# Where chunk 0 of the MLP passes into chunk 1: operands, sums, residual loads and stores in other places, and w2 at other addresses

## The chip, the cores and the metric

The kernel runs on one core of a Trainium2 chip. The metric is the device time of one execution in microseconds. Before the change it is 1118.84 us, the median of three runs (1115.59, 1118.84 and 1119.8 us).

## What is computed

A Performer attention layer feeds a two-layer MLP with a residual. The reference, cut to what matters:

```python
# q, k, v: 8 batches, 8 heads, 576 tokens, 64 wide; omega: 128 x 64
h = x @ omega.T - sum(x * x) / 2          # for x = scaled q and scaled k
phi = exp(h - max(h)) / sqrt(128)
attn = (q_p @ (k_p.T @ v)) / (q_p @ sum(k_p) + 1e-6)
x = attn                                   # 8 x 576 x 512
u = x + ((x.T @ U) @ V).T                  # U: 576 x 32, V: 32 x 576
out = u + relu(u @ w_ch1) @ w_ch2          # 512 -> 2048 -> 512
```

The change touches only the last line.

## The kernel before

The MLP's 4608 tokens are 36 tiles of 128 rows, taken in nine **chunks**: chunk 0 has six tiles, chunks 1 to 7 have four, chunk 8 has two. Every float32 product is made of three TensorE matmuls, from a high and a low half of each operand (`split`: ScalarE rounds the high half, GpSimd or VectorE subtracts it to get the low half). TensorE (PE) is fed in an order that the program fixes, and so are the other engines in this part (`keep`).

**Chunk 0** runs in `whole_pass`: for each of the 16 blocks f of w1's 2048 columns, 24 matmuls of the first layer (L853, twelve of 512 columns and twelve of 256), then 18 of the second layer (L927: six tiles t, three matmuls each, against the tiles `w2h` and `w2l` of block f), while `each(f, i)`, for i = 0 to 3, hangs other work between them: the decoder that turns the stored float64 weights into float32 (`raw` loads, `mag`, `low`, `w2h`, `w2l`), and towards the end the preparation of chunk 1. Its inputs come from DRAM by `fetch` (`uraw`, four DMAs each on SP's queue), are turned by VectorE (L792, `uT`), summed by GpSimd (L822, `us`) and split into `ux`.

**Chunks 1 to 7** do the first layer with seven products in place of eight (`products`), over blocks p and p + 8 of w1: eight **passes** p = 0 to 7 for each chunk, each of seven **units** i = 0 to 6 of six 256-column matmuls (L901, into the banks X, Y, Z and W). The operands of a pass are seven `wx` tiles, made of blocks of w1 and of four VectorE sums `ws` (`Weights.add`); in chunk 1 they are made and stored to DRAM (`wx_dram`), later chunks load them back (`Again`). After a unit VectorE and ScalarE combine the banks (`near`, `far`) and apply the relu (`g`). The second layer of one pass is a generator `steps` of single matmuls (L927), which the next pass takes one by one between its own: 24 of them, and 18 in the first pass of chunk 1, which carries the end of chunk 0. Z is in bank p_m and W in p_kv; chunk 0 ends with its tiles 4 and 5 in the same two banks, so the `store` of these tiles (L946: VectorE adds the residual `u` that L941 loaded) has to be done before units 2 and 5 of the first pass. Unit 3 accumulates on unit 0's bank, unit 4 on unit 1's, unit 6 on unit 2's: unit 6 may start when VectorE has read Z for `far` (c22, after unit 4).

Before, `pairs` (the operands of chunk 1's first pass) get four of their seven tiles in chunk 0's f = 14 and one in f = 15, and the residuals of chunk 0 are loaded in f = 14. `between(i)`, after each unit, then adds one operand of the running pass and one of the next. `prepare`, the three GpSimd sums of the next chunk, stands whole behind unit 6 of pass 6.

In SBUF, w2's blocks 0 and 1 start at addresses with remainder 128 by 256 and its blocks 2 to 15 at remainder 224; `g`, `ux` and `wx` start at 160.

## Time and profile before

| | us |
|---|---|
| median of three runs | 1118.84 |
| the profiled execution's own time | 1119.64 |
| its span (first to last instruction) | 1117.9 |
| TensorE busy | 1088.7 (97%) |
| attention, up to about 360 us | 360.00 with 343.72 of TensorE busy |
| chunk 8, from 1062.7 us | 55.30 with 51.48 of TensorE busy |

The first and the last third of the profile are outside of the change. A matmul's busy time (0.28 us for 256 columns, 0.40 us for 512) is longer than the spacing of two starts, because matmuls overlap; time lost is therefore read from the spacing of starts. A bracket such as [2.34 <-DVE g L862] is the idle time ahead of an instruction and what ended it.

### The profile page before, as it was taken

The page shows a single profiled execution, that of the slowest core. Times are in us where ns is not written, and L with a number is a line of the kernel's source. Part 1 is how long each engine was busy: PE and PEld are TensorE (multiplying, and loading weights), DVE is VectorE, ACT ScalarE, POOL GpSimd, SP SyncE. Part 2 cuts the span into 40 slices and gives each one's busy share as a digit, 9 for nine tenths or more (in the row PEclk, how much of TensorE's full clock was granted, in tenths as well). Part 3 has the DMA queues.
Part 4 walks back from the last instruction along what each step waited for, and adds up shares of the span by engine and source line. Part 5 has one row for each costly group of instructions (what it writes and reads, how often), then busy time and mean ns, then how long its engine had stood idle before and what let it go on. Part 6 is the DMA issues. An engine that isn't in the chain of part 4 may idle for free.

```text
span 1117.9 us, 20593 instructions
## 1 busy us (share of the span) xinstructions
PE 1088.7 (97%) x7105; PEld 981.6 (88%) x7105; DVE 686.5 (61%) x1487; ACT 501.5 (45%) x1405; POOL 325.9 (29%) x337
## 2 busy tenths in 40 slices
PE   8999999999979998999999999999999999999998
PEld 7899889999958887789889989999999999999987
DVE  3899998988987775465743643644644644643421
ACT  4889879898845664334412212222222222222232
POOL 3446647445234554445400100100100100100133
PEclk8999999999989999989999999999999999999999
DMA  7779876674434462375695695785795795785510
GB/s 131 147 149 158 167 172 133 151 143 86 105 87 132 134 166 41 116 252 179 203 269 159 213 265 162 209 269 161 208 270 162 207 271 162 208 260 165 179 58 19
DMA packets 344360, 187.93 MB, mean 168 GB/s; under 512 B 275872, under 2 KB 275872, under 8 KB 344256
## 3 DMA queue, kind: packets, MB, share of 16 engines
q1 hardware_dynamic: 344192, 186.55, 63.2%
q8 instruction: 57, 0.93, 0.3%
q14 instruction: 47, 0.39, 0.1%
q0 software_dynamic: 64, 0.07, 0.0%
HBM read 152.99 MB, written 33.55 MB: 167 GB/s over the span
## 4 chain that ended last, share of the span: by engine, by line
PE 78%; DVE 9%; ACT 4%; DMA 3%; issue 2%; POOL 2%; SPq 2%; DVEq 0%; POOLq 0%; ACTq 0%
PE p_s L901 24%; PE p_n L927 16%; PE p_q L927 14%; PE p_p L853 4%; PE p_kv L442 4%; PE p_n L488 4%; PE p_p L530 3%; PE p_p L531 2%; PE p_p L532 2%; PE p_q L468 2%; POOL mag L164 1%; PE py L327 1%; DVE mag L143 1%; DVE mag L140 1%; SPq L383 1%
## 5 line engine op out<-in xcount | busy, mean ns | idle before, releaser
L901 PEld LDWEIGHTS p_s<-ux,wx 128*128 128x128 f32 x2352 | 443.2, 189 | 65.5 <-issue 3.1
L901 PE MATMUL p_s<-ux,wx 128*128 128x256 f32 x2352 | 472.3, 283 | 6.3 <-DVE far L706 3.5
L927 PE MATMUL p_n<-w2h,g 128*128 128x512 f32 x576 | 213.3, 396 | 0.0
L927 PE MATMUL p_q<-w2h,g 128*128 128x512 f32 x512 | 199.0, 394 | 0.0
L545 ACT ACTIVATE e<-p_p,nm 128x128 f32<-128x128 f32 x576 | 167.1, 386 | 36.2 <-DVE nm L538 28.4
L411 POOL TENSOR_TENSOR xl<-xT,xh 128x384 fp32r<-128x384 f32 x96 | 100.8, 1067 | 132.9 <-ACT xh L407 114.0
L822 POOL TENSOR_TENSOR us<-uT 128x512 f32<-128x512 f32 x14 | 19.2, 1370 | 338.5 <-DVE uT L792 338.5
L861 ACT ACTIVATE g<-far 128x256 fp32r<-128x256 f32 x112 | 46.8, 418 | 157.1 <-DVE far L706 157.1
L706 DVE TENSOR_TENSOR near<-p_s,near 128x256 f32<-128x256 f32 x168 | 70.3, 419 | 74.7 <-PE p_s L901 71.8
L927 PE MATMUL p_n<-w2l,g 128*128 128x512 f32 x288 | 113.8, 395 | 0.0
L703 POOL TENSOR_TENSOR wx<-w1f,wx 128x256 fp32r<-128x256 f32 x88 | 68.6, 795 | 153.6 <-DMA u<-u_dram 81.6
L538 DVE TENSOR_REDUCE nm<-p_p 128x4 f32<-128x512 f32 x144 | 98.0, 681 | 23.6 <-PE p_p L532 16.0
L927 PEld LDWEIGHTS p_n<-w2h,g 128*128 128x128 f32 x576 | 105.4, 190 | 4.5
L861 ACT ACTIVATE g<-p_s 128x256 fp32r<-128x256 f32 x56 | 21.6, 385 | 186.1 <-PE p_s L901 186.1
L853 PEld LDWEIGHTS p_p<-ux,wx 128*128 128x128 f32 x576 | 87.9, 193 | 15.0 <-DVE g L862 3.8
L927 PE MATMUL p_q<-w2l,g 128*128 128x512 f32 x256 | 100.7, 393 | 0.0
L853 PE MATMUL p_p<-ux,wx 128*128 128x256 f32 (+1 forms) x576 | 97.6, 323 | 3.0 <-DVE g L862 3.0
L862 DVE SCALAR_TENSOR_TENSOR g<-p_s,g 128x256 fp32r<-128x256 f32 x56 | 23.7, 424 | 124.9 <-ACT g L861 124.6
L927 PEld LDWEIGHTS p_q<-w2h,g 128*128 128x128 f32 x512 | 96.6, 189 | 3.0
L530 PE MATMUL p_p<-omh,xh 128*128 128x256 f32 x288 | 93.2, 324 | 2.0 <-ACT e L545 1.7
L862 DVE SCALAR_TENSOR_TENSOR g<-far,g 128x256 fp32r<-128x256 f32 x112 | 49.8, 445 | 54.2 <-ACT g L861 54.2
L532 PE MATMUL p_p<-omh,xl 128*128 128x256 f32 x288 | 81.7, 284 | 0.0
(122 smaller groups left out, 1882.9 us busy)
## 6 DMA issues: line engine op xcount, KB each, us to landing
wx<-wx_dram SPq DMA_DIRECT2D x336, 256.0 KB, 3.3
raw<-in_moe_w_ch_dram SPq DMA_DIRECT2D x32, 512.0 KB, 4.0
wx_dram<-wx SPq DMA_DIRECT2D x56, 256.0 KB, 2.4
u_dram<-ut SPq DMA_DIRECT2D x36, 256.0 KB, 2.2
u<-u_dram SPq DMA_DIRECT2D x34, 256.0 KB, 4.4
out_dram<-u SPq DMA_DIRECT2D x34, 256.0 KB, 3.2
kt<-in_k_dram SPq DMA_DIRECT2D x120, 72.0 KB, 2.8
qt<-in_q_dram SPq DMA_DIRECT2D x120, 72.0 KB, 2.7
```

The costliest lines, as they stand in the source:

```text
L411: nc.gpsimd.tensor_tensor(out=self.xl[-1], in0=self.turned, in1=f32(self.xh[-1]), op=ALU.subtract)
L530: nc.tensor.matmul(o, part.xh[g][:, ts], oh, start=True, stop=False)
L532: nc.tensor.matmul(o, part.xl[g][:, ts], oh, start=False, stop=True)
L538: nc.vector.tensor_reduce(out=self.nm[:, :n], in_=self.pp[:, :n], axis=AX.X, op=ALU.max, negate=True)
L545: nc.scalar.activation(out=self.e[:, j, :], in_=self.pp[:, j, :], func=AF.Exp, bias=self.nm[:, j : j + 1])
L703: keep(rest.tensor_tensor(out=hl[:, 1], in0=x, in1=f32(hl[:, 0]), op=SUBTRACT))
L706: keep(nc.vector.tensor_tensor(out=out, in0=a, in1=b, op=op))
L853: nc.tensor.matmul(ph, l, r, start=(cc + i == 0), stop=(cc == NC - 1 and i == 2))
L861: keep(nc.scalar.activation(out=g[:, 0, ts], in_=x, func=AF.Relu))
L862: keep(nc.vector.scalar_tensor_tensor(out=g[:, 1, ts], in0=x, scalar=0.0, in1=f32(g[:, 0, ts]), op0=ALU.max, op1=ALU.subtract))
L901: tc.keep_in_program_order(nc.tensor.matmul(o, l, r, start=(i in (0, 1, 2, 5) and k + j == 0), stop=(k == 1 and j == 2), skip_group_check= ...
L927: tc.keep_in_program_order(nc.tensor.matmul(po, l, r, start=(begin and n + i == 0), stop=(end and n == len(fs) - 1 and i == 2)))
```

## The change

Eight edits, none of which alters the arithmetic or the number of matmuls:

- `fetch` of chunk 1's last two inputs in f = 9 and 10 is at i = 2 in place of i = 0.
- The six residual loads of chunk 0 go from f = 14 to f = 12 (four) and f = 13 (two).
- Six tiles of `pairs` are made at i = 1 and 3 of f = 12, 13 and 14; the seventh follows after unit 0.
- `Weights.add` makes its sums 1 and 2 with tile 0 (not 1), sum 3 with tile 3 (not 4), sum 4 with tile 4 (not 6).
- `prepare` can be called in parts: in pass 6 its sums come after units 2, 5 and 6.
- The second layer's matmuls: an even unit takes three inside and one behind it (before: two and two), an odd unit two and one, at other places.
- `store` of a tile of chunks 0 to 7 isn't done when its last matmul has been taken, but put in a list, of which `between` takes one after each unit.
- `warm` is allocated ahead of w2's first blocks, and a new tile `edge` of 64 bytes at the end of the right side: blocks 0 and 1 move up by 32 bytes, blocks 2 to 15 and the other tiles of the right side (`omh`, `oml`, `su`, `sv`, `x` of the attention, and `uraw`) down by 64. All of w2 then has remainder 160 by 256, as `g` has. `edge` gets one memset on VectorE.

```diff
+    warm = const.tile([P, 1], F32, name="warm")
     w2s = {f: [const.tile([P, DM], F32R, name=f"w2{a}{f}") for a in "hl"] for f in range(AHEAD)}
...
+    edge = ctx.enter_context(tc.tile_pool(name="edge", side="right", bufs=1)).tile([P, 16], F32, name="edge")
...
         def add(self):
             i, blk = len(self.ops), self.block
             if i == 0:
-                x = blk(0, 0)
-            elif i == 1:
                 self.sum(1, blk(0, 1), blk(1, 1), ADD)
                 self.sum(2, self.s[1], blk(0, 0), SUBTRACT)
...
             elif i == 3:
-                x = blk(1, 0)
+                self.sum(3, blk(0, 0), blk(0, 1), SUBTRACT)
             elif i == 4:
...
                 self.sum(4, blk(1, 0), self.s[2], SUBTRACT)
...
-                        if (k, j) in ((0, 1), (1, 0)):
+                        if 3 * k + j in ((1, 3) if i % 2 else (0, 2, 3)):
                             take(steps, 1)
...
-                if end:
+                if end and self.c < NCH - 1:
+                    stores.append(lambda t=t, po=po: self.store(t, po))
+                elif end:
                     self.store(t, po)
...
-        if i == 0 and f in (6, 7, 9, 10):
+        if (f, i) in ((6, 0), (7, 0), (9, 2), (10, 2)):
             nxt.fetch()
+        if f == 12:
+            one.residual((4, 5, 0, 1)[i])
...
+        if f == 13 and i > 1:
+            one.residual(i)
...
-        if f == 14:
+        if 12 <= f < 15 and i % 2:
             pairs.add()
-            one.residual((4, 5, 0, 1)[i])
-            if i > 1:
-                one.residual(i)
...
-            while len(pairs.ops) < 5:
-                pairs.add()
...
             def between(i):
-                take(steps, 2 - i % 2)
-                if p == 6 and i == 6 and not short:
-                    nxt.prepare()
+                take(steps, 1)
...
+                if p == 6 and not short and i in (2, 5, 6):
+                    nxt.prepare([(2, 5, 6).index(i)])
...
+                if stores:
+                    stores.pop(0)()
```

Three places in the order of instructions. First SP's queue in chunk 0, where the last loads of stored weights (`raw`) meet the inputs of chunk 1 (`uraw`). Before:

```order
L173 DMA raw<-in_moe_w_ch_dram 128x1024 x4
L355 DMA uraw<-u_dram_67 32x16x32 x4
L173 DMA raw<-in_moe_w_ch_dram 128x1024
L355 DMA uraw<-u_dram_67 32x16x32 x4
L754 DMA wx_dram_0_5456<-wx 128x512
```

After:

```order
L174 DMA raw<-in_moe_w_ch_dram 128x1024 x5
L356 DMA uraw<-u_dram_67 32x16x32 x8
L942 DMA u<-u_dram_66 128x512 x2
L749 DMA wx_dram_0_5461<-wx 128x512
```

The third `uraw` fetch now stands behind the last `raw` load, and the residual loads `u` ahead of the operands' stores.

Second VectorE (DVE) in the first pass of chunk 1, from the `near` after unit 1 to the `far` after unit 4, which frees Z for unit 6 (`u` and `more` rows are chunk 0's stores). Before:

```order
L706 TENSOR_TENSOR near<-p_s,near 128x256
L946 TENSOR_TENSOR u<-p_kv,u 128x512
L703 TENSOR_TENSOR ux<-us,ux 128x512
L706 TENSOR_TENSOR ws<-w1f,ws 128x256
L946 TENSOR_TENSOR u<-p_n,u 128x512
L706 TENSOR_TENSOR ws<-w1f 128x256
L706 TENSOR_TENSOR ws<-ws,w1f 128x256
L946 TENSOR_TENSOR u<-p_n,u 128x512
L862 SCALAR_TENSOR_TENSOR g<-p_s,g 128x256
L703 TENSOR_TENSOR ux<-uT,ux 128x512
L946 TENSOR_TENSOR more<-p_q,more 128x512
L706 TENSOR_TENSOR near<-p_s,near 128x256
```

After:

```order
L708 TENSOR_TENSOR near<-p_s,near 128x256
L705 TENSOR_TENSOR ux<-us,ux 128x512
L947 TENSOR_TENSOR u<-p_kv,u 128x512
L947 TENSOR_TENSOR u<-p_n,u 128x512
L861 SCALAR_TENSOR_TENSOR g<-p_s,g 128x256
L705 TENSOR_TENSOR ux<-uT,ux 128x512
L708 TENSOR_TENSOR ws<-w1f 128x256
L947 TENSOR_TENSOR u<-p_n,u 128x512
L708 TENSOR_TENSOR near<-p_s,near 128x256
L708 TENSOR_TENSOR far<-p_s,near 128x256
```

Between the two `near` there were ten instructions and are now seven; one store and three sums have left, one sum has come in.

Third VectorE again, at the end of chunk 1's pass 6 and the start of pass 7 (`far` and `g` are the last combination of pass 6, the `ux` rows are chunk 2's). Before:

```order
L862 SCALAR_TENSOR_TENSOR g<-near,g 128x256
L706 TENSOR_TENSOR far<-p_s,near 128x256
L862 SCALAR_TENSOR_TENSOR g<-far,g 128x256
L706 TENSOR_TENSOR ws<-w1f,ws 128x256
L703 TENSOR_TENSOR ux<-uT,ux 128x512
```

After:

```order
L861 SCALAR_TENSOR_TENSOR g<-far,g 128x256
L787 STREAM_TRANSPOSE uT<-uraw 128x512
L708 TENSOR_TENSOR ws<-w1f,ws 128x256
L708 TENSOR_TENSOR near<-p_s,near 128x256
L861 SCALAR_TENSOR_TENSOR g<-near,g 128x256
L708 TENSOR_TENSOR far<-p_s,near 128x256
L861 SCALAR_TENSOR_TENSOR g<-far,g 128x256
L705 TENSOR_TENSOR ux<-uT,ux 128x512
```

The sum that feeds the last `wx` tile stood behind pass 6's last `g`; it now stands four rows further ahead.

More of the change, by code (lines that the diff above doesn't have):

```diff
@@ L84, in performer_mlp_kernel @@
     idle = const.tile([P, P], F32, name="idle")
-    warm = const.tile([P, 1], F32, name="warm")
+    edge = ctx.enter_context(tc.tile_pool(name="edge", side="right", bufs=1)).tile([P, 16], F32, name="edge")
     mix = ctx.enter_context(ExitStack())
@@ L570, in performer_mlp_kernel @@
     nc.vector.memset(warm, 0.0)
+    nc.vector.memset(edge, 0.0)
     nc.scalar.activation(out=warm, in_=warm, func=AF.Exp)
@@ L734, in add @@
             if i == 0:
-                x = blk(0, 0)
-            elif i == 1:
                 self.sum(1, blk(0, 1), blk(1, 1), ADD)
                 self.sum(2, self.s[1], blk(0, 0), SUBTRACT)
-                x = self.s[2]
-            elif i == 2:
-                x = self.s[1]
             elif i == 3:
-                x = blk(1, 0)
+                self.sum(3, blk(0, 0), blk(0, 1), SUBTRACT)
             elif i == 4:
-                self.sum(3, blk(0, 0), blk(0, 1), SUBTRACT)
-                x = self.s[3]
-            elif i == 5:
-                x = blk(1, 1)
-            else:
                 self.sum(4, blk(1, 0), self.s[2], SUBTRACT)
-                x = self.s[4]
+            x = (
+                lambda: blk(0, 0), lambda: self.s[2], lambda: self.s[1], lambda: blk(1, 0),
+                lambda: self.s[3], lambda: blk(1, 1), lambda: self.s[4],
+            )[i]()
             self.ops.append(weight_tile())
@@ L822, in sum, with prepare @@
             keep(nc.gpsimd.tensor_tensor(out=self.s[i], in0=a, in1=b, op=op))
-        def prepare(self):
-            self.sum(1, self.block(0, 1), self.block(0, 0), SUBTRACT)
-            self.sum(2, self.block(1, 1), self.s[1], SUBTRACT)
-            self.sum(3, self.block(1, 1), self.block(0, 1), SUBTRACT)
+        def prepare(self, part=(0, 1, 2)):
+            for i in part:
+                if i == 0:
+                    self.sum(1, self.block(0, 1), self.block(0, 0), SUBTRACT)
+                elif i == 1:
+                    self.sum(2, self.block(1, 1), self.s[1], SUBTRACT)
+                else:
+                    self.sum(3, self.block(1, 1), self.block(0, 1), SUBTRACT)
         def add(self):
@@ L947, in store @@
             keep(nc.sync.dma_start(out=rows_out[r : r + P, :], in_=u))
+    stores = []
     def take(steps, n=None):
@@ L1081, in performer_mlp_kernel @@
     take(steps)
+    while stores:
+        stores.pop(0)()
     def each(f, i):
```

## Prediction

> **What bounds the kernel now.** I read the page's busy table first, then busy time by stage (start and end, length, then for each engine its busy time and its count, granted clock, DMA share, GB/s).
>
> ```profile
> PE 1088.7 (97%) x7105; PEld 981.6 (88%) x7105; DVE 686.5 (61%) x1487; ACT 501.5 (45%) x1405; POOL 325.9 (29%) x337
> 360.00:464.50 104.50, 101.55 (x507) 85.16 (x506) 66.25 (x103) 52.69 (x109) 50.57 (x48) 1.00 0.39 103
> 464.50:562.00 97.50, 91.24 (x552) 80.96 (x551) 63.49 (x123) 39.56 (x107) 50.67 (x61) 0.96 0.65 220
> 562.00:1062.70 500.70, 500.70 (x3141) 451.75 (x3141) 237.73 (x514) 114.87 (x279) 30.11 (x24) 1.00 0.72 210
> ```
>
> TensorE (PE) is the bound. From 562 to 1062.7 us it has no idle time at all, so nothing hung beside it there can be gained from; idle time stands in chunk 0 (2.95 us) and chunk 1 (6.26 us). The copy `near` (L879) runs once in each pass and serves as a pace: first the passes after chunk 1, then chunk 1 with the copy of the next one.
>
> ```profile
> L879 ACT COPY near<-p_s x47: 352/373/374, 569.6 to 1053.9; 128x256 f32<-128x256 f32 x47
> L879 ACT COPY near<-p_s x9: 356/367/373, 466.0 to 560.6; 128x256 f32<-128x256 f32 x9
> ```
>
> Undisturbed, a pass takes (1053.9 - 569.6) / 46 = 10.53 us. Chunk 1's eight took 94.6 where 84.2 would do, or 82.8, as the first has 18 second-layer matmuls in place of 24 (6 x 0.23 us). Of these 11.8 us, 1.4 is only the ninth copy coming late (10.53 - (569.6 - 560.6) = 1.5): some 10.3 us are lost. The timeline of PE, ScalarE (ACT), VectorE (DVE), GpSimd (POOL) and SP's queue, in three pieces, shows where.
>
> ```profile
> 420.46 1.92 SPq L355 DMA_DIRECT2D uraw<-u_dram  x4
> 422.49 5.52 DMA raw<-in_moe_w_ch_dram
> 427.28 0.39 PE L927 MATMUL p_kv<-w2h,g 128*128 128x512 f32 x1
> 428.09 0.66 ACT L123 ACTIVATE low<-raw 128x512 int32<-128x512 uint32 x1 [2.27 <-DMA raw<-in_moe_w_ch_dram]
> 430.02 4.47 PE L853 MATMUL p_p<-ux,wx 128*128 128x512 f32 x24 [2.34 <-DVE g L862]
> 438.29 0.39 PE L927 MATMUL p_kv<-w2h,g 128*128 128x512 f32 x1
> 439.30 3.04 PE L853 MATMUL p_p<-ux,wx 128*128 128x512 f32 x12 [0.61 <-DVE g L862]
> ```
>
> In chunk 0 ACT waited 2.27 us for the last `raw` load, with the relu that PE needed queued behind it. The load was issued only after four `uraw` DMAs. Starts are 2.74 and 1.01 us apart where a second-layer matmul takes 0.23: **3.3 us lost** (2.51 + 0.78).
>
> ```profile
> 467.42 0.39 PE L927 MATMUL p_n<-w2h,g 128*128 128x512 f32 x1
> 467.95 0.48 PE L901 MATMUL p_s<-ux,wx 128*128 128x256 f32 x2
> 472.72 0.28 PE L901 MATMUL p_s<-ux,wx 128*128 128x256 f32 x1
> 474.09 0.85 PE L901 MATMUL p_s<-ux,wx 128*128 128x256 f32 x5 [1.09 <-POOL ux L703]
> 475.12 0.42 DVE L862 SCALAR_TENSOR_TENSOR g<-p_s,g 128x256 fp32r<-128x256 f32 x1 [0.20 <-ACT g L861]
> 475.63 0.69 DVE L703 TENSOR_TENSOR ux<-uT,ux 128x512 fp32r<-128x512 f32 x1
> 476.24 0.69 DVE L946 TENSOR_TENSOR more<-p_q,more 128x512 f32<-128x512 f32 x1
> 476.84 0.42 DVE L706 TENSOR_TENSOR near<-p_s,near 128x256 f32<-128x256 f32 x1
> 477.29 0.42 DVE L706 TENSOR_TENSOR far<-p_s,near 128x256 f32<-128x256 f32 x1
> 477.86 2.05 PE L901 MATMUL p_s<-ux,wx 128*128 128x256 f32 x8 [2.91 <-DVE far L706]
> 480.13 0.63 PE L901 MATMUL p_s<-ux,wx 128*128 128x256 f32 x2
> 480.56 0.63 PE L927 MATMUL p_n<-w2l,g 128*128 128x512 f32 x1
> 483.44 0.40 PE L927 MATMUL p_n<-w2h,g 128*128 128x512 f32 x1
> 425.00:440.00 15.00, 12.04 (x57) 1.00 0.16 34
> 475.00:485.00 10.00, 7.14 (x31) 0.66 0.98 362
> ```
>
> In the first pass of chunk 1 PE lost 0.30 us (467.42 to 467.95), 1.25 (472.72 to 474.09, less 0.12 for a 256-column matmul) and about 3.1 (2.91 idle and the overlap of two matmuls) ahead of unit 6, which waits for `far`, the last of five VectorE instructions in a row. From 477.86 to 483.44 two starts are 0.43 us apart in place of 0.23; the last two rows (length, PE busy, granted clock, DMA) have the granted clock at 0.66 there, where the 2.34 us stop in chunk 0 left it at 1.00. Half of 5.58 us is 2.8 us. In sum **7.4 us**.
>
> ```profile
> 546.06 1.29 POOL L822 TENSOR_TENSOR us<-uT 128x512 f32<-128x512 f32 x1
> 547.56 1.51 DVE L706 TENSOR_TENSOR ws<-w1f,ws 128x256 f32<-128x256 f32 x1
> 549.15 0.40 ACT L702 CAST wx<-ws 128x256 fp32r<-128x256 f32 x1 [2.86 <-DVE ws L706]
> 549.98 0.36 ACT L879 COPY near<-p_s 128x256 f32<-128x256 f32 x1
> 550.39 0.50 PE L901 MATMUL p_s<-ux,wx 128*128 128x256 f32 x2 [1.29 <-ACT near L879]
> 552.33 0.50 PE L901 MATMUL p_s<-ux,wx 128*128 128x256 f32 x2 [0.26 <-DVE near L706]
> 556.24 0.50 PE L901 MATMUL p_s<-ux,wx 128*128 128x256 f32 x2 [0.58 <-DVE far L706]
> ```
>
> At pass 7 a sum on VectorE took 1.51 us beside POOL's `us` sums (0.42 elsewhere), ACT waited 2.86 us for it, and PE for ACT: 1.29 + 0.26 + 0.58 and 0.17 of overlap each, **2.7 us**. 3.3 + 7.4 + 2.7 = 13.4 us are at stake; chunk 1's 10.1 agree with the 10.3 by the copies.
>
> **The change, part by part.** *The third fetch behind the last `raw`.* The load no longer queues behind 1.92 us of `uraw` issues and their transfers. At 422.49 - 1.92 = 420.6 plus the 5.52 us that it took, it lands at 426.1, the latest, two microseconds ahead of 428.09. Chunk 1's inputs are wanted by the transposes two f's later (some 16.8 us), so nothing new waits. The 0.78 us stop follows the same chain with lateness carried on; I take 2.9 of 3.3 us (at least 2.0).
>
> *Operands and residuals earlier.* Two ACT casts, two POOL halves, two sums for each f from 12 to 14, and six loads: PE had no gap from 439.3 to 467.4 and each f gives 8.4 us (24 and 18 matmuls, the 4.19 and 3 x 1.40 rows below) for about 3 us of such work on any engine, so nothing. If that cover failed, one operand of each of three f's would be late by half a 1.29 us GpSimd instruction, 2 us. The seventh tile and the next pass's first now share unit 0; the latter waits for unit 1 to leave its slot, with ACT's casts for units 4 and 5 behind it, both with over 2 us to spare.
>
> *What is late next in the first pass.* By 0.12 and 0.23 us a matmul the units start at 0, 1.6, 3.0, 4.7, 6.1, 7.7 and 8.4 us. The stores of tiles 4 and 5 come at once, as their residuals are there: the 0.30 goes. GpSimd's half for unit 5 stands behind that for unit 3 and three `wx` halves: 2.6 + 1.29 + 3 x 0.7 + 1.29 = 7.3 (0.7 for half the columns), 0.4 ahead of its unit: the 1.25 goes, barely. VectorE after unit 3 (6.1): ACT's relu 0.4, then `g`, `ux`, `ws`, a store, `near` and `far`. By the rows these take 0.42, or 0.61 start to start (475.63 to 476.24), with ACT's cast of 0.6 ahead of `ux`: `far` ends near 9.5, so unit 6 stops for **1.1 us** in place of 3.1. The next pass's fourth second-layer matmul needs the `g` of c21, behind one more store: 0.45. Each `ws` or `ux` that runs beside POOL can grow as the 1.51 row did; I add 0.35. So 1.9 us come back (0.9 with `far` as early as ACT allows, to 3.4 with `ux` and `ws` both grown by 0.75), and 5.5 of 7.4 go.
>
> The trace has PE stopped for 2.34 us at clock 1.00 and for 1.09 + 2.91 us with five matmuls between ahead of 0.66. One wait of 1.1 to 1.9 is below the first, so I let the clock's 2.8 go. The Trainium skill ("TensorE: Matmul & The Clock Gate", Part 1) halves the clock after an idle window of about 3.4 us. Here 2.91 us, ended by work at half pace, sufficed with 1.09 ahead of it, so the trace is stricter than that sentence; by its rule alone a 3 us stop would be harmless.
>
> *Sum 4 earlier and `prepare` spread, pass 6.* The last `wx` cast finds its sum two units old, so ACT's `near` is on time; POOL's three sums still meet VectorE after units 5 and 6, and one `g` may grow by the 1.1 us that the sum did, inside the 1.4 us of a unit. 2.4 of 2.7 us go (at least 1.3). Chunks 2 to 7 had no idle time there and gain nothing.
>
> *Other places for second-layer matmuls, and stores from a list.* 25 are taken per pass as before; four neighbouring pairs per pass are parted. The spacing below is 0.23 us whether a pair or a first-layer matmul follows: nothing, within the 0.005 us that two starts resolve, for 8 changed neighbours in 56 passes: 2.2 us both ways. A store moves by at most one unit (1.4 us), its bank is wanted a pass later; on SP it is passed by one `wx` load. Nothing.
>
> ```profile
> 443.77 1.40 PE p_n L927 x6
> 447.97 4.19 PE p_p L853 x24
> 1084.38 1.44 PE p_p L853 x12
> 300.93 0.28 PE L530 MATMUL p_p<-omh,xh 128*128 128x256 f32 x1
> 301.28 0.27 PE L468 MATMUL p_q<-ident,e 128*128 128x128 f32 x1
> ```
>
> *Addresses.* No row tries this placement for w2. Nearest is L853, whose operands share remainder 160: (4.19 - 1.44) / 12 = 0.229 us for 512 columns (1.44 is twelve of 256, chunk 8's row), against 1.40 / 6 = 0.233 for w2. Over the 384 matmuls that run in rows of six or more (16 x 18 and 16 x 6) that is 1.6 us gained, and 7 if the other 1344 gained as much. Against it, attention's 256-column matmuls, whose operands are 64 bytes off and now meet, take (301.28 - 300.93) / 3 = 0.117, and L853's 0.120: 0.003 on 864 is 2.6 us lost, and 7.8 if w2 lost as much. The two nearest rows pull against each other, 1.6 and 2.6, so I take 0, with 7 gained and 7.8 lost as ends. The same page (Part 2, step 1) says that loading weights takes no read bandwidth from the running matmul: by that the edit is worth 0; neither the 0.004 nor the 0.003 is explained by it. *The memset* of `edge` is one short instruction, below a `ws` of 0.42 us, ahead of the first inputs; some rows of the start change places with it: 0, within 0.7.
>
> Sum: 2.9 + 5.5 + 2.4 = 10.8 us. The profiled execution's own time is 1119.64, which gives 1108.8; that run lies 0.8 above the median of 1118.84, which gives 1108.0. I forecast **1108.2 us** (from 1119.0). Its own bounds: 2.0 + 4.0 + 1.3 = 7.3 up to 3.3 + 6.5 + 2.7 = 12.5 us, and 2.2 of spacing both ways, so 1104 to 1114.
>
> **The rivals.** *VectorE stays the bound of the first pass.* If `far` is over 2.3 us late, the clock drops again: 2.3 + 2.8 us back and only 2.3 gone. Total 2.9 + 2.3 + 2.4 = 7.6, less 1.0 for the next pass's wait on `g`: 6.6, so 1112.4. For it: six stores are still in that pass. Against: its sums have left.
> *The addresses pay*: 1.6 to 7 more, 1101 to 1107.
> *The reorder does not reach chunk 0's stop*, because the load was late for its buffer and not for the queue: 2.9 stay, 1111. Against it: its issue follows the fourth `uraw` at once.
> *Slower: operands at one remainder collide.* TensorE reads the moving w2 while it loads the next `g`. Attention's 2.6 us come with it, and each of the 1728 second-layer matmuls pays: at (10.8 - 2.6) / 1728 = 4.7 ns the gain is gone, at 8 ns the kernel is 5.6 us slower, 1124.6. For it: the 3 ns of attention. Against it: L853 at one remainder isn't slower than w2 apart, and 8 ns is more than any two rows differ by.
>
> **How the numbers follow.** Forecast 0.57, VectorE 0.16, addresses pay 0.14, chunk 0 0.08, slower 0.05. A measurement of this kernel can tell 0.5% (5.6 us) from no change. Faster than 1113.2: forecast, addresses and chunk 0 whole, and a third of the VectorE case, 0.84; the rest of that case and half of the last, 0.13, is the same; 0.03 slower. The range, 1101.5 to 1115, leaves out the collision and the tails.
>
> **What would show it.** Right: no PE wait near f = 10 above 1 us, clock 1.00 throughout the first passes, one wait of about 1 us for `far` ahead of the first unit 6, none for `near` in pass 7, copies still 10.53 us apart later on. Wrong: granted clock under 0.9 there, or a changed spacing of L927 or L901, which 56 passes would multiply.

## The result, and the profile after

The changed kernel takes 1108.79 us (median of 6 runs, 1108.08 to 1111.88) where the kernel before took 1117.71 beside it (6 runs, 1115.52 to 1119.80): a ratio of 0.9928, 95% interval 0.9915 to 0.9942. The forecast was 1108.2. The total is right; the terms that make it up are not, and most of this section and the next is about that. (The forecast counted from 1119.0 and not from 1117.71: 10.8 us of gain were forecast and 8.9 measured.)

The busy table of the changed kernel, and its stages cut at the same times as before (start and end, length, then busy time and count of PE, weight load, VectorE, ScalarE, GpSimd, then granted clock, DMA share, GB/s):

```profile
PE 1082.9 (98%) x7105; PEld 976.8 (88%) x7105; DVE 681.9 (62%) x1488; ACT 501.5 (45%) x1405; POOL 330.6 (30%) x337
360.00:464.50 104.50, 102.16 (x518) 86.17 (x518) 70.48 (x108) 54.49 (x114) 54.72 (x52) 1.00 0.46 125
464.50:562.00 97.50, 95.20 (x590) 85.40 (x589) 61.30 (x129) 38.64 (x106) 50.21 (x56) 0.98 0.66 220
562.00:1062.70 500.70, 500.70 (x3142) 450.26 (x3141) 236.23 (x511) 115.42 (x281) 31.90 (x27) 1.00 0.71 207
```

TensorE is still the bound and its idle time in the second and third piece fell from 9.2 to 4.6 us. Two things say that this isn't the whole story: chunk 0 still has idle time, and PE's busy time fell by 5.8 us although the same 7105 matmuls run. Part of that is clock, part is that matmuls stand closer together. The copy `near` as a pace, later passes and then chunk 1:

```profile
L878 ACT COPY near<-p_s x46: 355/372/373, 571.6 to 1044.1; 128x256 f32<-128x256 f32 x46
L878 ACT COPY near<-p_s x9: 356/372/373, 477.2 to 561.1; 128x256 f32<-128x256 f32 x9
```

A later pass takes (1044.1 - 571.6) / 45 = 10.50 us, 0.03 less than before. By the starts of the matmuls in the two traces, the program divides like this (a stage runs from its first matmul to the next stage's; chunk 8 to the start of its last one; the third line is a second profiled execution of the changed kernel, an experiment below):

| us | attention | chunk 0 | chunk 1 | its passes 0, 1, 7 | chunks 2 to 7 | chunk 8 |
|---|---|---|---|---|---|---|
| before | 328.42 | 136.17 | 93.15 | 14.69, 12.36, 13.47 | 505.28 | 50.76 |
| changed | 327.42 | 134.63 | 86.97 | 12.04, 11.39, 11.04 | 504.01 | 50.33 |
| changed, again | 328.28 | 134.04 | 85.83 | 11.41, 10.98, 11.04 | 504.01 | 50.33 |

Attention ends at 327 to 328 us here and not at about 360, and chunk 8, like everything else, has tiles at new addresses: neither end of the profile lies outside of the change. The first block of chunk 0, f = 0, runs partly at half clock, until 333.1 us before, 332.7 in the changed kernel and 331.8 in its second execution; so chunk 0 is also counted from f = 2 on, below.

**Chunk 0.** The chain of waits of the changed kernel, and below it the timeline's PE rows (start, duration, what ran, and in brackets idle time and its releaser):

```profile
420.53 0.61 DVE mag L144
421.20 4.62 DMA raw<-in_moe_w_ch_dram
425.91 0.66 ACT low L124
426.57 0.50 ACT g L860
427.09 0.53 DVE g L861
427.83 4.49 PE L852 MATMUL p_p<-ux,wx 128*128 128x512 f32 x24 [1.45 <-DVE g L861]
437.12 4.46 PE L852 MATMUL p_p<-ux,wx 128*128 128x512 f32 x24 [0.69 <-DVE g L861]
```

The step before the load is no longer SyncE's queue but `mag L144`, VectorE's last read of the buffer that the load fills. The queue is free and the load still leaves only at 421.20: 1.3 us earlier than before by the clocks of the two traces, 0.5 us by the sums of the f ahead (VectorE's L862 at 417.48 then, L861 at 416.64 now). It lands at 425.8, and ScalarE's `low` (L124), which waits for it, has the sums' relu (L860) queued behind it. The two stops are 1.45 and 0.69 us, together 0.8 less than before, not 2.9 (1.72 and 0.73 in the second execution: 0.5 less).

**Chunk 1, first pass.** The same timeline on VectorE, GpSimd (POOL) and PE, from unit 3 to unit 6:

```profile
468.41 1.30 POOL L705 TENSOR_TENSOR ux<-us,ux 128x512 fp32r<-128x512 f32 x1
469.06 1.20 DVE L705 TENSOR_TENSOR ux<-uT,ux 128x512 fp32r<-128x512 f32 x1
469.67 1.18 POOL L705 TENSOR_TENSOR wx<-ws,wx 128x256 fp32r<-128x256 f32 x1
470.18 0.95 DVE L708 TENSOR_TENSOR ws<-w1f 128x256 f32<-128x256 f32 x1
471.05 0.68 DVE L947 TENSOR_TENSOR u<-p_n,u 128x512 f32<-128x512 f32 x1
471.65 0.41 DVE L708 TENSOR_TENSOR near<-p_s,near 128x256 f32<-128x256 f32 x1
472.10 0.42 DVE L708 TENSOR_TENSOR far<-p_s,near 128x256 f32<-128x256 f32 x1
472.67 1.83 PE L900 MATMUL p_s<-ux,wx 128*128 128x256 f32 x7 [2.04 <-DVE far L708]
```

The waits for unit 5's operand and for the early stores are gone, as forecast. The stop ahead of unit 6 is 2.04 us and not 1.1: `ux` and `ws` run beside GpSimd and start 1.12 and 0.87 us ahead of their successors, not 0.61 each. Then the clock. In every trace of this case the stretches at half clock are 3.41 us long or a multiple of that, and begin and end on one grid of such steps (in this profile they begin at 15.29, 319.07 and 472.67 us, 89 and 45 steps apart; the last, cut off by the end of the program, aside). Steps of the grid around the stop (columns as above), first in this profile, then in the second execution of the same kernel, with its stop:

```profile
469.26:472.67 3.41, 1.37 (x11) 1.11 (x9) 3.23 (x5) 0.19 (x2) 2.45 (x3) 1.00 0.93 347
472.67:476.08 3.41, 3.41 (x13) 3.22 (x14) 2.60 (x6) 1.31 (x4) 1.57 (x2) 0.50 0.80 298
476.08:479.50 3.42, 3.42 (x23) 3.08 (x23) 2.39 (x6) 2.00 (x6) 2.31 (x4) 1.00 0.65 239
...
468.34:471.75 3.41, 2.56 (x17) 2.11 (x16) 2.83 (x4) 1.20 (x3) 3.41 (x4) 1.00 0.99 371
471.75:475.16 3.41, 2.21 (x15) 2.05 (x15) 2.71 (x7) 0.86 (x3) 1.26 (x2) 1.00 0.82 308
472.95 1.07 PE L900 MATMUL p_s<-ux,wx 128*128 128x256 f32 x7 [2.04 <-DVE far L708]
```

The stop is 2.04 us at the same place in both. In the first it lies within one step of the grid (470.63 to 472.67), and the next step runs at half clock; in the second the grid cuts it into 0.85 and 1.19 us of idle time, and the clock stays. That is the 1.0 us by which their passes 0 and 1 differ (23.43 and 22.39). The last section sets all profiles side by side.

**Pass 7** has one wait left, for `far`, in place of three:

```profile
547.51 0.39 PE L900 MATMUL p_s<-ux,wx 128*128 128x256 f32 x1 [0.26 <-DVE far L708]
```

### The profile page after: what moved, and what is told of

It is laid out like the page before. It is cut to its first block, busy times and chain, and to the rows that moved or that the text cites. A ratio compares the mean times of both kernels' runs of the same rounds, so it can differ in the third digit from the quotient of the medians.

```text
span 1107.4 us, 20580 instructions
## 1 busy us (share of the span) xinstructions
PE 1082.9 (98%) x7105; PEld 976.8 (88%) x7105; DVE 681.9 (62%) x1488; ACT 501.5 (45%) x1405; POOL 330.6 (30%) x337
## 4 chain that ended last, share of the span: by engine, by line
PE 74%; DVE 10%; DMA 4%; ACT 3%; SPq 3%; issue 3%; POOL 2%; DVEq 0%; POOLq 0%; ACTq 0%
PE p_s L900 23%; PE p_n L926 16%; PE p_q L926 14%; PE p_p L852 4%; PE p_n L489 3%; PE p_kv L443 3%; SPq L384 2%; PE p_p L531 2%; PE p_q L469 2%; PE p_p L532 2%; PE p_p L533 2%; PE py L328 1%; POOL mag L165 1%; DVE mag L144 1%; DVE mag L141 1%
## 5 line engine op out<-in xcount | busy, mean ns | idle before, releaser
L900 PE MATMUL p_s<-ux,wx 128*128 128x256 f32 x2352 | 494.1, 280 | 2.3 <-DVE far L708 2.3
L900 PEld LDWEIGHTS p_s<-ux,wx 128*128 128x128 f32 x2352 | 438.4, 189 | 44.6 <-issue 2.2
L926 PE MATMUL p_n<-w2h,g 128*128 128x512 f32 x576 | 219.7, 396 | 0.0
L926 PE MATMUL p_q<-w2h,g 128*128 128x512 f32 x512 | 195.2, 392 | 0.0
L860 ACT ACTIVATE g<-far 128x256 fp32r<-128x256 f32 x112 | 46.9, 418 | 171.5 <-DVE far L708 171.5
L926 PEld LDWEIGHTS p_n<-w2h,g 128*128 128x128 f32 x576 | 108.9, 189 | 9.3
L861 DVE SCALAR_TENSOR_TENSOR g<-p_s,g 128x256 fp32r<-128x256 f32 x56 | 23.7, 423 | 140.5 <-ACT g L860 140.5
L860 ACT ACTIVATE g<-p_s 128x256 fp32r<-128x256 f32 x56 | 21.7, 387 | 185.7 <-PE p_s L900 185.7
L861 DVE SCALAR_TENSOR_TENSOR g<-far,g 128x256 fp32r<-128x256 f32 x112 | 49.5, 442 | 54.3 <-ACT g L860 54.3
```

The source lines that it names most:

```text
L860: keep(nc.scalar.activation(out=g[:, 0, ts], in_=x, func=AF.Relu))
L861: keep(nc.vector.scalar_tensor_tensor(out=g[:, 1, ts], in0=x, scalar=0.0, in1=f32(g[:, 0, ts]), op0=ALU.max, op1=ALU.subtract))
L900: tc.keep_in_program_order(nc.tensor.matmul(o, l, r, start=(i in (0, 1, 2, 5) and k + j == 0), stop=(k == 1 and j == 2), skip_group_check= ...
L926: tc.keep_in_program_order(nc.tensor.matmul(po, l, r, start=(begin and n + i == 0), stop=(end and n == len(fs) - 1 and i == 2)))
```

## The experiments

Lengths of stages, f's and passes are worked out from matmul starts, as in the table; they come from one profiled execution each. "Ratio" is to the kernel before, in the same series of runs.

### The addresses and the places of the second-layer steps

Three runs went together. `a_addr` puts the addresses of the changed kernel back:

```diff
     w1f = const.tile([P, NC, DF], F32, name="w1f")
-    warm = const.tile([P, 1], F32, name="warm")
...
     idle = const.tile([P, P], F32, name="idle")
-    edge = ctx.enter_context(...).tile([P, 16], F32, name="edge")
+    warm = const.tile([P, 1], F32, name="warm")
```

> The changed kernel with the addresses put back: warm stands behind w2 of f=0 and 1 again and there is no edge tile, so w2 stands at remainder 128 or 224 by 256 and g at 160. Theory (addresses pay where w2 and g meet): against the changed kernel each f of chunk 0 and of chunk 8 is longer by 18 x 6 ns = 0.1 us or more, chunk 0 by 1 to 1.7 us, chunk 8 by 0.4, chunks 2 to 7 by up to 1.3 if the steady pass returns from 10.50 to 10.52 us; attention by up to 1.0; the whole is 1110.5 to 1113. Rival (the order of the steps and the spread work gave this time, addresses nothing, as predicted): every stage within 0.2 us of the changed kernel, the whole 1108.8 +- 0.7.

`b_addr` makes only this edit, the other way round, in the kernel before:

> The kernel before with the new addresses alone (warm ahead of w2 of f=0 and 1, the edge tile under the others), its order untouched. Theory (addresses pay): chunk 0 shorter by 0.8 to 1.7 us, chunk 8 by 0.4, chunks 2 to 7 by up to 1.3; attention, whose tiles move by 64 bytes, 1.0 shorter if it is the addresses that shorten it; the whole 2 to 4 us below the kernel before. Rival (addresses nothing): every stage within 0.2 us of the kernel before, the ratio 1.000 +- 0.001.

`a_take` puts back the places of the steps:

```diff
-                        if 3 * k + j in ((1, 3) if i % 2 else (0, 2, 3)):
+                        if (k, j) in ((0, 1), (1, 0)):
...
-                take(steps, 1)
+                take(steps, 2 - i % 2)
```

> The changed kernel with the old places of the second-layer steps inside the units of products (after the inner indices 1 and 3, and 2 - i % 2 between the units). Theory (the places shortened the steady pass): a pass of chunks 2 to 7 returns from 10.50 to 10.52 us or more, the stage grows by 1.2 us, chunk 0 and chunk 8 stay. Rival (the addresses did it, the places nothing): a pass stays at 10.50 us and the stage at 504.0, the whole at 1108.8 +- 0.7. Second rival (the places feed the clock or the first pass of chunk 1): only chunk 1 moves, by over 0.3 us.

Measured: `a_addr` 1113.16 us, ratio 0.9967 (0.9954 to 0.9980); `b_addr` 1118.07, ratio 1.0006 (0.9992 to 1.0021); `a_take` 1112.16, ratio 0.9948 (0.9929 to 0.9968). The timeline gives the length of one f of chunk 0, where no work waits, as the distance of two blocks of 24 first-layer matmuls. Two rows each of before, `a_addr`, changed, `b_addr`:

```profile
377.15 4.35 PE L853 MATMUL p_p<-ux,wx 128*128 128x512 f32 x24
385.55 4.35 PE L853 MATMUL p_p<-ux,wx 128*128 128x512 f32 x24
...
367.77 4.35 PE L850 MATMUL p_p<-ux,wx 128*128 128x512 f32 x24
376.17 4.35 PE L850 MATMUL p_p<-ux,wx 128*128 128x512 f32 x24
...
359.36 4.32 PE L852 MATMUL p_p<-ux,wx 128*128 128x512 f32 x24
367.62 4.32 PE L852 MATMUL p_p<-ux,wx 128*128 128x512 f32 x24
...
362.98 4.32 PE L855 MATMUL p_p<-ux,wx 128*128 128x512 f32 x24
371.24 4.32 PE L855 MATMUL p_p<-ux,wx 128*128 128x512 f32 x24
```

8.40 with the old addresses and 8.26 with the new, whatever the rest of the program. Chunk 8 is 50.77 us in `a_addr` and 50.33 in `b_addr`. So addresses are not worth 0 there: over the eleven f's of chunk 0 that wait for nothing in either kernel the changed one gains 1.3 us, and in chunk 8 0.4. (What becomes of the 1.3 is told with the stops of chunk 0, below.)

The steady pass depends on both edits. `near` in the later chunks of `a_addr`, `b_addr` and `a_take`:

```profile
L876 ACT COPY near<-p_s x46: 353/372/373, 570.9 to 1047.3; 128x256 f32<-128x256 f32 x46
L881 ACT COPY near<-p_s x47: 353/373/375, 569.2 to 1054.5; 128x256 f32<-128x256 f32 x47
L878 ACT COPY near<-p_s x46: 357/373/374, 573.0 to 1047.7; 128x256 f32<-128x256 f32 x46
```

| chunks 2 to 7, us (one pass) | w2 at 224 or 128 | w2 at 160 |
|---|---|---|
| old places | 505.28 (10.53), before | 506.40 (10.55), `b_addr`; 506.41 (10.55), `a_take` |
| new places | 508.20 (10.59), `a_addr` | 504.01 (10.50), changed |

Each edit alone makes the stage longer (by 1.1 and 2.9 us); both together make it 1.3 shorter. For `a_take` that is the expected direction and twice the size, for `a_addr` three times what was expected. `a_take` lands on `b_addr` to 0.01 us, so of all the other edits only the places matter there. Why they interact isn't shown: the spacing of matmuls that touch no w2 changes too, and nothing in the trace names a cause.

The pace isn't set by the program alone. Passes 2 to 6 of chunk 1 take 10.50 us each in the changed kernel's first execution and 10.48 in its second; in `a_far` (below), whose chunks 2 to 7 are the changed kernel's, the pace goes from 10.50 to 10.48 in chunk 3 and stays there (503.38 us), while six other executions have 504.00 to 504.16. So 0.02 us of a pass, 1.0 us of the stage, need not be an edit's. The 1.1 and the 1.3 of the table are about as large as that; the 2.4 of `a_take` and the 2.9 and 4.2 of `a_addr` are beyond it.

`a_addr`'s chunk 0 as a whole was not longer than the changed kernel's (134.45) since its stops are shorter (0.49 and 0.59 us); the expectation erred in taking them as fixed. It is no chance of one execution: the two kernels below with w2 away from 160 have 0.57 and 0.64, and 0.94 and 0.63. `b_addr` gains 1.9 us in chunk 0 and 0.4 in chunk 8 and yet its total is that of before: it gives 1.1 back in chunks 2 to 7, and the profiled execution 3.7 in attention, whose length varies (last section). Its chunk 1 is 2.2 us shorter, with stops of 1.33 and 1.18 us in the first pass where before had 1.09 and 2.91; whether the addresses did that, one profile can't say.

Is it equality that pays, or the place? Two kernels change only the size of `edge`, so that w2 of f from 2 on stands at 192 or at 96 while g stays at 160, and w2 of f=0 and 1 at 160:

```diff
-    edge = ...tile([P, 16], F32, name="edge")
+    edge = ...tile([P, 8], F32, name="edge")
```

> The changed kernel with 32 bytes on the right side in place of 64: w2 of f from 2 on stands at remainder 192 by 256, g and w1 at 160. Theory (equal remainders of the operands are what pays): an f of chunk 0 takes 8.35 us or more, as with 224, and a pass 10.55 or more. Rival (224 and 128 are bad, any other place is good): 8.26 and 10.50, as with 160.

> The changed kernel with 128 bytes on the right side in place of 64: w2 of f from 2 on stands at remainder 96 by 256, 64 away from g as in the kernel before, on the other side. Theory (equal remainders pay): 8.35 us or more for an f of chunk 0 and 10.55 or more for a pass, as with 224. Rival (the remainder by 64, 32 for 96, 160 and 224 alike, can't be it; but a place below 224 can): 8.26 and 10.50, as with 160.

The first blocks of `a_edge8`, then two later ones, and the same pair of `a_edge32`:

```profile
343.48 4.32 PE L852 MATMUL p_p<-ux,wx 128*128 128x512 f32 x24
351.74 4.32 PE L852 MATMUL p_p<-ux,wx 128*128 128x512 f32 x24
...
368.49 4.35 PE L852 MATMUL p_p<-ux,wx 128*128 128x512 f32 x24
376.88 4.36 PE L852 MATMUL p_p<-ux,wx 128*128 128x512 f32 x24
...
367.08 4.33 PE L852 MATMUL p_p<-ux,wx 128*128 128x512 f32 x24
375.46 4.33 PE L852 MATMUL p_p<-ux,wx 128*128 128x512 f32 x24
```

Within one execution of `a_edge8` the first distance, while w2 of the first f's is used, is 8.26 us, and it is 8.39 later; with 96 it is 8.38. So 96, 192 and 224 all cost 0.12 to 0.13 us an f and only 160, the remainder of g, doesn't. That speaks for equality; but g itself was never moved, so that 160 is simply a good place for w2 isn't ruled out, and a period of 128 bytes would fit these places as well as one of 256. In the steady pass it isn't all or nothing: 10.50 us at 160, 10.52 at 96, 10.54 at 192, 10.59 at 224; the 10.55 or more that was expected for 96 and 192 is wrong. The totals of these two (1110.15 and 1109.33, 2 runs each) can't be told from the changed kernel's.

### Chunk 0: the place of the loads, or the work ahead of the relu

```diff
-        if (f, i) in ((6, 0), (7, 0), (9, 2), (10, 2)):
+        if i == 0 and f in (6, 7, 9, 10):
```

> The changed kernel with the operand loads of f=9 and 10 issued at i=0 again, ahead of the decoder's loads of i=0 and 1. Theory (the decoder's last load waits for its buffer, which VectorE frees at 421.1 us, and the queue adds only the 1.3 us that the loads of f=10 take): the last load is issued at 422.4 in place of 421.2, the stop before the sums of f=11 grows from 1.6 to some 2.6 us, chunk 0 by 0.8 to 1.2 us, nothing else moves; the whole 1109.6 to 1110.0. Rival (the place of the loads never mattered, chunk 0 gained by its addresses alone): chunk 0 within 0.2 us of the changed kernel's 134.6. The prediction as it stands on record would want 2 us or more.

Ratio 0.9945 (0.9924 to 0.9966), 1111.83 us. The buffer's last read, the load's issue (SyncE's queue), its flight in the chain of waits, and PE:

```profile
422.19 0.67 DVE L144 SCALAR_TENSOR_TENSOR mag<-raw,mag 128x512 uint32<-128x512 uint32 x1
423.41 0.42 SPq L174 DMA_DIRECT2D raw<-in_moe_w_ch_dram  x1
423.41 5.24 DMA raw<-in_moe_w_ch_dram
430.66 6.04 PE L852 MATMUL p_p<-ux,wx 128*128 128x512 f32 x24 [2.54 <-DVE g L861]
```

The buffer is free at 422.86 and the load goes 0.55 us later; it then flies 5.24 us beside the operands' loads, against 4.62 and 4.90 in the two executions of the changed kernel. Together 0.9 to 1.2 us is what the place of the loads costs; the rest of the lateness is the buffer's. The stop is 2.54 us, as expected, and the 24 matmuls after it take 6.04 in place of 4.49 since the clock fell, which no expectation had. Chunk 0 takes 135.11 us.

Six profiles side by side, in us from the first matmul of f = 2 (343.65 before, 342.84 in the changed kernel), show what the stop is made of:

| | w2 at 160 | f = 11 starts | last load leaves | lands | stop | chunk 0 ends |
|---|---|---|---|---|---|---|
| before | no | 75.47 | 78.84 | 84.36 | 2.34 | 120.94 |
| `b_addr` | yes | 74.83 | 78.84 | 83.74 | 2.20 | 119.95 |
| `a_fetch` | yes | 74.73 | 78.80 | 84.04 | 2.54 | 120.81 |
| `a_addr` | no | 75.47 | 78.35 | 82.43 | 0.49 | 119.06 |
| changed | yes | 74.76 | 78.36 | 82.98 | 1.45 | 119.21 |
| changed, again | yes | 74.74 | 78.33 | 83.23 | 1.72 | 119.44 |

The new place of the fetches lets the load leave 0.5 us sooner, with old and new addresses alike, and mostly fly shorter (4.08 to 4.90 us against 4.90 to 5.52). The new addresses bring TensorE to f = 11 0.7 us sooner and leave the start of the load where it is. This, and a landing that varies by 0.8 us within the new order, make the stop short where only the order is new and longer again where both are. (In `a_addr` `low` waits a last 0.1 us, behind the landing, for GpSimd's `mag`.) In the new order chunk 0 gains nothing from the addresses: 119.06 without, 118.71 to 119.44 with them in the five executions that share the changed kernel's chunk 0 (`a_far`, `a_prep` and `a_take` are the others, with stops of 0.98 to 1.22). The 1.3 us of the undisturbed f's go into the stops and into f = 9 and 10.

If the buffer sets the landing, the stop can only go by having less ahead of the relu. `a_dec` leaves out one decoder step at each of two places; they follow later:

```diff
-        advance(decoder, 1 + (i < 3), True)
+        advance(decoder, 1 + (i < 3) - (f == 9 and i > 1), True)
```

> The changed kernel with one step of the decoder less at i=2 and at i=3 of f=9, so that ScalarE's read of the last loaded piece (L124) and the copy of w2 of f=15 stand behind the sums' relu and not ahead of it. Theory (the sums of chunk 0 wait because a piece that is late for its buffer stands ahead of them on ScalarE; where the loads of the operands stand matters little): f=11 of chunk 0 falls from 9.0 to 11.3 us (as the runs so far have it) to 8.3 to 8.7, the next from 9.29 to 8.3 to 9.3; chunk 0 is 132 to 133 us, the rest unchanged. Rival (the queue or the transfers are what is late, whatever stands ahead): f=11 stays above 9 us.

f=11 and f=12 take 9.23 and 9.15 us (changed kernel: 10.23 and 9.29, 10.50 and 9.29), chunk 0 133.30; the waits are 0.44 and 0.58 us. The direction is the theory's, the size half of it; 9.23 is also above the 9 us that the rival had set, so this run alone doesn't decide between them. The total (1109.44, ratio 0.9932, 0.9907 to 0.9957) doesn't show it. In that order another step of the decoder stood ahead of the relu, on ScalarE for GpSimd and on VectorE for ScalarE, which leads to `a_best2` below.

### Chunk 1

`a_far` takes two instructions from ahead of `far`:

```diff
-                if new and len(pairs.ops) == 7:
+                if new and len(pairs.ops) == 7 and not (c == 1 and p == 0 and i == 3):
```

> The changed kernel, where in chunk 1's first pass the unit 3 prepares no operand of the next pass's w1 (a 0.95 us sum on VectorE and a 1.18 us subtraction on GpSimd go from ahead of the read of Z to behind unit 4). Theory (the stop before unit 6 is VectorE's chain of five operations, and what follows is the clock's): the stop falls from 2.04 us to 0.7 to 1.2, the clock does not fall, passes 0 and 1 together go from 23.4 us (22.4 to 23.4 in the runs so far) to 20.5 to 21.5. Rival (the clock falls after any stop at this place): the stop falls but the spacing of 0.43 us stays for some 3 us and the two passes take over 21.8. Second rival (the operand is late for the second pass): a new stop at the start of the second pass, over 0.5 us.

VectorE and PE at the same place:

```profile
471.74 1.20 DVE L705 TENSOR_TENSOR ux<-uT,ux 128x512 fp32r<-128x512 f32 x1
472.86 0.68 DVE L947 TENSOR_TENSOR u<-p_n,u 128x512 f32<-128x512 f32 x1
474.48 1.07 PE L900 MATMUL p_s<-ux,wx 128*128 128x256 f32 x7 [1.17 <-DVE far L708]
```

`far` is 0.87 us earlier and the stop 1.17; the clock stays. Passes 0 and 1 take 10.54 and 11.09 us, 21.63, a tenth above the expected range and 0.8 and 1.8 below the changed kernel's two executions. 1107.77 us, ratio 0.9927 (0.9903 to 0.9951). The second pass has no stop above 0.23 us, so neither rival fits.

`a_prep` puts the three sums of `prepare` back behind unit 6 of pass 6:

```diff
-                if p == 6 and not short and i in (2, 5, 6):
-                    nxt.prepare([(2, 5, 6).index(i)])
+                if p == 6 and not short and i == 6:
+                    nxt.prepare()
```

> The changed kernel with the three sums of prepare together behind unit 6 of pass 6 again. Theory of the prediction (the sums spread over units 2, 5 and 6 take away most of the loss of pass 7): pass 7 of chunk 1 returns from 11.04 us to 13 or more. Rival (the fourth sum, which now stands with its tile, and not prepare, made pass 7 long): pass 7 stays at 10.8 to 11.1. In the later chunks the passes stay at 10.50.

```profile
543.58 1.75 POOL L817 TENSOR_TENSOR us<-uT 128x512 f32<-128x512 f32 x1
546.26 0.39 PE L900 MATMUL p_s<-ux,wx 128*128 128x256 f32 x1 [0.92 <-DVE near L708]
550.48 0.39 PE L900 MATMUL p_s<-ux,wx 128*128 128x256 f32 x1 [0.91 <-DVE far L708]
```

Pass 7 takes 12.87 us (11.04 with the spread, 13.47 before), a little under the 13 that was expected, so the spread is worth 1.8 of the 2.4 us. The other 0.6 fits the fourth sum's new place, which was not tried alone. The later passes did not stay at 10.50: they take 10.48 (chunks 2 to 7 503.04 us), the other pace of above. 1111.02 us, ratio 0.9950 (0.9932 to 0.9967).

### A faster version

`a_best` joins `a_dec` and `a_far` and pops no store behind unit 3:

```diff
-                if stores:
+                if stores and i != 3:
```

> The changed kernel with the decoder's later steps, with no operand of the next pass's w1 at unit 3 of chunk 1's first pass, and with no store popped behind unit 3. Theory: the stop before unit 6 is below 0.5 us, the first two passes take 19.9 to 20.9 us, chunk 0 132 to 133; the whole is 3.5 to 5 us below the changed kernel, 1104 to 1106 on a chip where that takes 1109. Rival: VectorE's work only moves, and the lost time shows as stops before later units or at the second pass; the whole within 1.5 us of the changed kernel.

1106.21 us, ratio 0.9912 (0.9891 to 0.9933). By the ratios that is some 2 us below the changed kernel (0.9928 and 0.9934 in its two series) and not 3.5 to 5, and the intervals overlap. The stop is 0.57 us and the two passes 9.94 and 11.12, 21.06 in all, both just outside what was expected; chunk 0 132.95, with 9.16 us left in f=11 and f=12. The next kernel takes the decoder's steps further back:

```diff
-        advance(decoder, 1 + (i < 3) - (f == 9 and i > 1), True)
+        advance(decoder, 1 + (i < 3) if i < 2 or f not in (9, 10) else 0, True)
```

> The last kernel (no operand of the next pass's w1 and no store at unit 3) with the decoder's steps at i=2 and i=3 left out in f=9 and in f=10, which come later. Theory (what was left of the stops in chunk 0 is still a wait of the decoder ahead of the relu, on ScalarE for GpSimd's sum and on VectorE for ScalarE): f=11 and f=12 fall from 9.16 us each to 8.3 to 8.8, chunk 0 to 131.5 to 132.5; 2 to 5 us below the changed kernel beside it. Rival (the pieces are now late where they are used, or the steps only move): a stop before the second-layer matmuls of f=13 to 15, or f=12 stays above 9; chunk 0 above 132.8.

Beside it ran the changed kernel itself:

> The changed kernel itself, as the pace for the runs beside it. Theory (the clock falls or not after the same 2.04 us stop, by where the stop lies to something that this program doesn't set): passes 0 and 1 together take 22.4 us (no fall) or 23.4 (fall), chunk 0 133 to 135, chunks 2 to 7 503 to 504; the time 1107 to 1111. Rival (the fall belongs to this program): the clock falls as in the first profile and the two passes take 23.2 to 23.6 us.

Changed kernel 1109.44 us (1108.15 to 1111.78, 6 runs, ratio 0.9934, 0.9917 to 0.9952); `a_best2` 1104.42 (1102.90 to 1105.76, 4 runs, ratio 0.9884, 0.9866 to 0.9903). No idle time over 0.1 us is left in chunk 0 behind f = 0: f=11 and f=12 take 8.61 and 8.26 us, the chunk 131.42. In chunk 1 the wait for `far` is

```profile
467.35 1.07 PE L900 MATMUL p_s<-ux,wx 128*128 128x256 f32 x7 [0.58 <-DVE far L708]
```

and chunks 2 to 8 are the changed kernel's to 0.01 us. The profiled spans differ by 5.5 us, 2.6 of it in chunk 0, 1.3 in chunk 1 and 1.5 in attention, whose program is the same in both; so some 3.9 of these 5.5 us are the edits'. It beats both kernels.

## Why the prediction was right in the sum and not in its steps

- **Chunk 0's stop, 2.9 us forecast, 0.5 to 0.8 found** (up to 1.3 in the five executions of its program). The step that failed is "The load no longer queues behind 1.92 us of `uraw` issues". It no longer queues, and waits for its buffer instead until 421.1, so it leaves 0.5 us sooner; "422.49 - 1.92 = 420.6" took the queue as the only thing that held it. The landing forecast for "the latest", 426.1, was right by the clock (425.8 and 426.1), and still the stop stayed: "two microseconds ahead of 428.09" compares two traces by the clock, as if TensorE arrived when it did before. It reaches f = 11 1.5 us sooner (417.60, not 419.12), 0.7 of it through the addresses that were priced at 0. With the old addresses the stop is 0.49 us. The rival given 0.08 had the buffer right, but not that the stop stays whatever else is done. `a_dec` and `a_best2` show what else it was made of: decoder steps ahead of the relu on two in-order engines.
- **First two passes, 5.5 us forecast, 3.6 and 4.7 found.** The waits for unit 5 and for the early stores went as said. The term that was too small is the growth beside GpSimd: "I add 0.35" where `ux` and `ws` grew by 0.77 together. The stop was 2.04 us, and 0.57 to 1.17 with those operations taken away. "I let the clock's 2.8 go" took the 2.34 us stop of chunk 0 as a bound that a shorter stop can't break. That stop was cut by the grid into 1.01 and 1.33 us; the stop of 2.04 lay within one step in one of the two executions, and the clock fell, for about 1.0 us. The rival that VectorE stays the bound had the clock right half the time and its price too high.
- **Pass 7, 2.4 us forecast, 2.43 found.** `a_prep` shows that the spread of `prepare` carries most of it.
- **Operands and residuals earlier, 0.** Nothing contradicts it; they were not tried alone.
- **Places of the second-layer steps, 0 forecast.** Alone with the new addresses they are worth 2.4 us (`a_take`), and with the old ones they cost 2.9. "25 are taken per pass as before; four neighbouring pairs per pass are parted" was right and "nothing" wrong: 0.05 us of a pass, on 48 passes, just outside of the 2.2 us both ways that the prediction allowed for.
- **Addresses, 0 forecast.** The first of the two rows that were set against each other was the better guide: 0.004 us for a 512-column matmul gave 1.6 us on the matmuls that run in rows, and the undisturbed f's of chunk 0 gained 1.3, chunk 8 0.4. What it left out is that chunk 0 would hand its part on to the stop. The Trainium skill ("TensorE: Matmul & The Clock Gate", Part 2, step 1) was read as saying that the edit is worth 0; the trace doesn't agree with that reading, since an f is 8.26 us at equal remainders and 8.38 to 8.40 at three unequal ones.
- **Slower by collision.** Ruled out for chunks 0 and 8; in chunks 2 to 7 the new addresses cost 1.1 us with the old places, no more than the pace varies by. Attention's 2.6 us can't be seen: its length varies by more from one execution to the next.

In the sum: chunk 0 1.5 us, chunk 1 6.2, chunks 2 to 8 1.7, attention 1.0 that is not the change's; the forecast had 2.9, 7.9, 0 and 0. 1.4 us too much in chunk 0 and 1.7 too much in chunk 1 stood against 1.7 of address and order that were not forecast, and attention's 1.0. That the time came out within 0.6 us of the forecast is luck, for this reason and because the forecast counted from 1119.0, 1.3 above the 1117.71 that the kernel before took beside the changed one. Of the five signs of being right that the prediction named, four did not come in the first profile: a wait near f = 10 is above 1 us (1.45), the clock fell to 0.50 in the first passes, the wait for `far` is 2.04 us and not about 1, and the copies are 10.50 us apart and not 10.53. Only the wait for `near` in pass 7 is gone, as it said.

## What to carry to other kernels

A load that leaves right behind another on its queue may have a second reason for its time: find when its buffer is last read before counting on the queue, and then look at what is queued behind its reader, since moving that is worth more than the load. Compare two traces from a common point near the place and not by their clocks: what feeds a wait and what ends it can both move. Price VectorE work beside GpSimd by the longest row of that tile and not by the shortest. A change of some nanoseconds in the spacing of matmuls is worth testing by itself and together with the order, and against what the same program varies by: here each alone lost in the steady state and both together gained, and two of these four differences are no larger than that.

## What the runs showed of the hardware that was not expected

- **A stop halves the clock by how much of one 3.41 us step it fills, and not by its length.** The grid of these steps lies elsewhere in each execution. From f = 1 of chunk 0 to chunk 7, in all 14 profiles, a step at full clock was followed by one at half clock whenever TensorE was idle for 1.91 us of it or more: 2.04 in the changed kernel, `a_dec` and `a_fetch`, 1.91 in chunk 0 of `a_fetch` (its stop of 2.54), 2.36 in `b_addr` (stops of 1.33 and 1.18), 2.56 before. It never was with 1.55 us or less: the 2.34 us stop before is cut into 1.01 and 1.33, and those of 2.04 to 2.05 in the changed kernel's second execution, `a_edge8`, `a_edge32` and `a_prep` leave at most 1.49 in one step. Between them 1.81 us (`a_take`) was followed by it and 1.86 (`a_addr`) wasn't, so idle time, as the profile has it, isn't quite what counts. The Trainium skill ("TensorE: Matmul & The Clock Gate", Part 1) speaks of a free-running window of about 3.4 us that has to be idle. That it runs freely and its length fit the grid; that a whole window must be idle doesn't fit 1.81 us.
- **w2 at the remainder by 256 of g**, the other operand of a second-layer matmul, saves 0.12 to 0.13 us on an f's 18 second-layer and 24 first-layer matmuls against the remainders 96, 192 and 224, and 0.09 against 128, the old place of blocks 0 and 1 (f = 2 is 8.35 us long before). Whether it is equality or the place itself isn't shown, as g stayed at 160.
- **Attention's length varies from one execution to the next.** In executions whose attention is the same program the first matmul of chunk 0 starts at 326.8 to 332.1 us. The clock of the first 60 us doesn't settle it. `a_best2` (326.78), `a_prep` (330.82) and `a_take` (329.92), granted clock 1.00, 0.89 and 1.00:

```profile
0.00:60.00 60.00, 50.67 (x366) 45.45 (x367) 37.05 (x89) 41.02 (x132) 25.16 (x42) 1.00 0.74 136
0.00:60.00 60.00, 53.78 (x353) 49.52 (x353) 37.15 (x88) 39.10 (x124) 23.95 (x42) 0.89 0.75 138
0.00:60.00 60.00, 52.41 (x372) 47.17 (x373) 37.60 (x90) 41.21 (x132) 25.12 (x42) 1.00 0.75 137
```

What else makes the difference stays open. At up to 5.3 us it is larger than most of the effects here, which is why a stage is compared rather than the total.
